# A two-layer memory-attention and gMLP kernel: where a piece of filler stands beside the output projection, and which engine runs Newton's steps of a LayerNorm

## The chip, the cores and the metric

The kernel runs on one core of a Trainium2 chip. The metric is device time in microseconds (us): the median of three runs before the change is 1888.75 us (1885.54 to 1890.63). A core has a matrix engine (PE), a vector engine (DVE), an activation engine (ACT), GpSimd (POOL) and a queue engine for transfers (SP). Each takes its instructions in the order of its own list and waits for the others by semaphores.

## The reference

The input x has 2048 rows of 512 bf16 numbers. Two layers follow each other, and each layer is an attention block (A) and a gated MLP (B), both with a residual:

```
for s in range(64):                       # A: 64 segments of 32 rows, one after another
    h = concat([mem, x_ln[32*s : 32*s+32]])            # 8 memory rows + 32 tokens
    q, k, v = h @ Wq, h @ Wk, h @ Wv                   # 32 heads of 128
    p = softmax(where(mask, q @ k.T * scale, -1e9))    # 40 x 40 per head
    o = (p @ v) @ Wo
    mem, out[s] = o[:8], o[8:]            # memory rows feed the next segment
x = x + out

z  = gelu(LN(x) @ w_in)                   # B: 2048 x 1376
z1, z2 = z[:, :688], LN(z[:, 688:])       # LN over the 688 columns
x  = x + (z1 * (w_sp @ z2 + b_sp)) @ w_out    # w_sp is 2048 x 2048
```

The memory rows make the segments of A a chain: segment s+1 can't start its projections before the first 8 rows of segment s have been through Wo. The LayerNorm of the second half of z needs, for each row, a mean, a variance and 1/sqrt(variance + eps).

## The kernel before

Each layer calls `a_block` (line 476) and then `b_block` (line 224).

**Order.** PE, DVE and ACT run in the order of the program text: `ORDERED` (line 28) is handed to `manual_schedule` (lines 425, 508, 238). In `b_block` SP is in that set too (line 238). POOL is not in it, so there a scheduler places POOL's instructions among each other.

**Attention segments.** `segment` (line 650) does one segment: projections of q and k by `mm_chunk` (line 527, matmuls on line 531), scores (line 688), the value projection `v_mm`, the products with the values (line 711), the sums of the softmax in `psD` (line 763), and then the product of the memory rows with Wo, `wo_pass` (line 582), whose 128 small matmuls all have line 586. Before Wo, DVE must have scaled the memory rows into `uT` (line 773). After Wo, DVE puts the memory rows into the next segment's input (`build_hA`, line 638: a predicated copy on line 641 and a transpose on line 642), behind `tok_out(0)` (line 721) in its order; ACT copies Wo's result `pw` out for storage (line 647). The result `pw` and the sums `psM` share one bank of the accumulation memory (`accB`), and the filler uses the other (`accA`).

**Filler.** At five places of a segment `fill()` takes one piece of independent work for PE: after `v_mm(0)` (line 740), after `v_mm(1)` (747), after `psD` (765), in the middle of Wo (778) and after `build_hA` (791). There are two kinds of pieces:

- `b_units` (line 557), in three of every four segments (`j4` = 1, 2, 3) while a next block of four segments exists: six chunks of 16 matmuls project the token rows of the next block. Every second chunk is cut in four pieces of 4 matmuls, the others come whole, so that the 15 pieces fill the five places of three segments. With whole chunks at the last place and quarters at the first four, each segment does two chunks.
- `y_part` (line 602), in the segment with `j4` = 0 from the fifth block on: 8 matmuls of 128x128x512 (line 598, `wo_last`) that put older token rows through Wo. The first four places get one matmul each, the last gets four.

So 45 segments of a layer carry `b_units`, 12 carry `y_part`, and 7 carry nothing.

**The gMLP's projection phase.** `b_block` begins with 16 calls of `project` (line 258), one for each tile of 128 rows. A projection is 12 matmuls (line 263) into one of two `pz` buffers of the accumulation memory, two gelus on ACT (lines 265, 266) that free this buffer, and three statistics instructions on DVE (lines 270 to 272). After every second tile `norms` (line 274) computes 1/sqrt(var + eps) for the pair with `_rstd_dve` (line 116): a starting value by integer arithmetic on the bits and three Newton steps, 12 small DVE instructions on 128x2 or 128x4 numbers, and one more for `nb` = -mean/std (line 282). `normalise` (line 286, on ACT) scales the tile by these; it is called for the pair of tiles before the present one, right after `norms`. So ACT's order reads: gelus of tiles 4 and 5 stand behind the normalise of tiles 0 and 1, and so on by pairs.

**The late rows.** The last four tiles of 128 rows (12 to 15) have not got their residual when A ends. POOL issues transfers for them at the start of `b_block`: `late_load` (line 250) loads the old x and A's output (`y_load`, line 199) and calls `y_add` (line 208), which adds the two on POOL (line 210) and stores the sum (line 211). Ahead of them stand POOL's two transfers of `w_out` (lines 290, 291), which is first used in `finish` (line 354), after the projection phase. In `norms` of pairs 2 and 3 (`tt` = 5 and 7) DVE also takes statistics of two late rows each; these share the Newton steps (n = 4), and `y_norm` (line 216) normalises them on DVE and stores them to `xb_d` through POOL's queue (line 221). SP then reads them back transposed for the last four projections (`load_rows`, line 156).

Of the kernel before, what the change touches and what calls it, by code (L numbers as in the profile page):

```python
# [10 lines left out]
ALU = mybir.AluOpType  # L11
# [104 lines left out]
def _rstd_dve(nc, pool, out, var, n):  # L116

    t = pool.tile([P, n], F32, name=f"nt{n}")
    nc.vector.tensor_scalar(out=t[:], in0=var, scalar1=LN_EPS, scalar2=None, op0=ALU.add)
    b = pool.tile([P, n], mybir.dt.int32, name=f"nb{n}")  # L120
    nc.vector.tensor_scalar(out=b[:], in0=t[:].bitcast(mybir.dt.int32), scalar1=-0.5, scalar2=float(0x5f3759df), op0=ALU.mult, op1=ALU.add)
    nc.vector.tensor_scalar(out=t[:], in0=t[:], scalar1=-0.5, scalar2=None, op0=ALU.mult)
    y = b[:].bitcast(F32)
    for k in range(3):
        q = pool.tile([P, n], F32, name=f"nq{n}")
        nc.vector.tensor_tensor(out=q[:], in0=y, in1=y, op=ALU.mult)
        nc.vector.tensor_tensor(out=q[:], in0=q[:], in1=t[:], op=ALU.mult)
        o = out if k == 2 else pool.tile([P, n], F32, name=f"ny{n}", bufs=2)[:]
        nc.vector.scalar_tensor_tensor(out=o, in0=q[:], scalar=1.5, in1=y, op0=ALU.add, op1=ALU.mult)
        y = o  # L130
# [93 lines left out]
def b_block(tc, c, rows, front, xd, MV_out, RS_out, w_sp, w_out, S, first, out_final=None):  # L224
# [4 lines left out]
    with ExitStack() as ctx:  # L229
# [8 lines left out]
        ctx.enter_context(tc.manual_schedule(engines=ORDERED | {mybir.EngineType.SP}))  # L238
# [11 lines left out]
        def late_load(tb, x=None, o=None):  # L250
            rows.y_load(tb, first, nc.gpsimd, x=x, o=o)
            rows.y_add(tb, first, nc.gpsimd, nc.gpsimd)
# [21 lines left out]
        def norms(q, late):  # L274

            n = 4 if late else 2
            for k, tb in enumerate(late):
                rows.y_stats(tb, mv[q][:, 2 + k, :])
            rs[q] = zp.tile([P, 4], F32, name="rs")
            nb[q] = zp.tile([P, 2], F32, name="nb")  # L280
            _rstd_dve(nc, zp, rs[q][:, 0:n], mv[q][:, 0:n, 1], n)
            nc.vector.scalar_tensor_tensor(out=nb[q][:], in0=mv[q][:, 0:2, 0], scalar=-1.0, in1=rs[q][:, 0:2], op0=ALU.mult, op1=ALU.mult)
            for k, tb in enumerate(late):
                rows.y_norm(tb, mv[q][:, 2 + k, 0:1], rs[q][:, 2 + k:3 + k], nc.gpsimd)
# [5 lines left out]
        nc.gpsimd.dma_start(w_out_sb[:, 0:5, :], w_out[0:640, :].rearrange("(fc p) d -> p fc d", p=P))  # L290
        nc.gpsimd.dma_start(w_out_sb[0:48, 5, :], w_out[640:688, :])
# [4 lines left out]
        late_load(NT - 1, wl[:, 0, :], wl[:, 1, :])  # L296
        for tt in range(NT):
            project(tt)
            if tt in (7, 9, 11):
                load_wsp((tt - 7) // 2)  # L300
            if tt == 14:
                load_x(0)
            if tt % 2 == 1:
                if tt // 2 + 3 < NT // 2:
                    front.load_rows(tt // 2 + 3)
                norms(tt // 2, {5: (NT - 4, NT - 3), 7: (NT - 2, NT - 1)}.get(tt, ()))
                if tt > 1:
                    normalise(tt - 3)
                    normalise(tt - 2)
# [166 lines left out]
def a_block(tc, c, rows, front, MV_in, RS_in, MV_out, RS_out, wqkv, Wo, S, first):  # L476
# [6 lines left out]
    with ExitStack() as ctx:  # L483
# [73 lines left out]
        def b_units(tb, early=False):  # L557
            bs = blk_state[tb]

            for k, j in enumerate((0, 2, 1, 3, 4, 5)):  # L560
                ps = (accA if k % 2 == 0 or not early else accB).tile([P, 512], F32, name="psb")
                for kts in (((0,), (1,), (2,), (3,)), ((0, 1, 2, 3),))[k % 2]:
# [39 lines left out]
        def y_part(G, q):  # L602

            pwB = accA.tile([P, DM], F32, name="pwB")
            for k, _ in enumerate(wo_last(G, range(8 * q, 8 * q + 8), pwB)):
                if k < 4:
                    yield
# [42 lines left out]
        def segment(s, fill, spare1, spare2, tail):  # L650
# [125 lines left out]
            wo_pass(pw, uT_cur, range(0, H // 2))  # L776

            fill()
            wo_pass(pw, uT_cur, range(H // 2, H))
# [116 lines left out]
```

The softmax here doesn't subtract the row's maximum and nothing guards it: scores larger than these inputs give would overflow.

## Time and profile before

The page and the trace below are of one profiled execution. It took 1885.15 us by the same clock as the runs, 3.6 us under their median; the span from its first to its last instruction is 1883.4 us.

| | us | share of the span |
|---|---|---|
| median of 3 runs | 1888.75 | |
| profiled execution | 1885.15 | |
| its span | 1883.4 | 100% |
| PE busy | 1761.1 | 94% |
| DVE busy | 1162.7 | 62% |
| ACT busy | 1120.7 | 60% |
| POOL busy | 136.6 | 7% |
| matmuls of Wo (line 586), busy | 286.1 | 15% |
| matmuls of the gMLP's projections (line 263), busy | 79.4 | 4% |
| transfers | 125.8 MB, 67 GB/s on average | |

The granted TensorE clock is 0.994 of full speed over the span, so no time differs by clock.

How to read the lines in the next part: a timeline line gives the start and the length of a group of like instructions in microseconds, the engine, the line of the kernel, the operation with what it writes and reads, its tile and how many there were. A square bracket at its end is the idle time of the engine just before, with the engine and the line of what ended it. PE's matmuls are pipelined, so the lengths of groups overlap slightly; differences of starts are safer than lengths. "issue" as a cause means that the engine waited for nothing that the profile shows. Line 531 is in `mm_chunk` and so stands for several callers: the tile tells them apart (`psb` is the filler `b_units`, `psm` a segment's own projection of q and k).

### The profile page before, as it was taken

To read this page: it belongs to the slowest core of one execution; us is meant where nothing else is said; L and a number is where in the kernel's file an instruction comes from. 1 tells how busy PE (TensorE), PEld (TensorE's weight loads), DVE (VectorE), ACT (ScalarE), POOL (GpSimd) and SP (SyncE) were. 2 spreads that over 40 slices of the span, in tenths; PEclk is the share of its full clock that TensorE was granted. 3 is DMA by queue.
4 is the path that set the end of the run, shared out by engine and by line. 5 is a ranking of instruction groups with operands and counts; after the bars stand their busy time and mean duration, and the time that the engine had idled before them with its cause. 6 is when DMAs were issued, how large, how long until landed. Compare 5 with 4: busy or idle time off the path is not lost.

```text
span 1883.4 us, 94288 instructions
## 1 busy us (share of the span) xinstructions
PE 1761.1 (94%) x43572; PEld 1015.0 (54%) x43596; DVE 1162.7 (62%) x2700; ACT 1120.7 (60%) x2074; POOL 136.6 (7%) x289
## 2 busy tenths in 40 slices
PE   3999999999999999889989999999999999998898
PEld 1555555555555555545545555555555555555455
DVE  1666666676667666674346666666766676665822
ACT  1666676666667666652036666666666666665600
POOL 5000000000000000032010000000000000001200
PEclk9999999999999999999999999999999999999999
DMA  9100000021002111267940000001210121114696
GB/s 348 46 19 19 20 18 18 21 68 38 17 17 72 42 25 39 78 154 162 207 139 21 21 21 21 21 21 32 80 35 21 32 83 39 29 43 124 141 186 130
DMA packets 189267, 125.80 MB, mean 67 GB/s; under 512 B 135896, under 2 KB 164328, under 8 KB 188872
## 3 DMA queue, kind: packets, MB, share of 16 engines
q1 hardware_dynamic: 167016, 71.01, 16.3%
q0 software_dynamic: 10560, 34.07, 5.5%
q10 hardware_dynamic: 11296, 14.70, 2.6%
q8 instruction: 340, 5.57, 1.2%
q14 instruction: 55, 0.45, 0.1%
HBM read 59.29 MB, written 33.56 MB: 49 GB/s over the span
## 4 chain that ended last, share of the span: by engine, by line
PE 84%; DVE 5%; DMA 4%; issue 3%; ACT 2%; POOL 0%; SPq 0%; ACTq 0%; DVEq 0%; POOLq 0%
PE psm L531 24%; PE pw L586 13%; PE psV L531 12%; PE psb L531 8%; PE pg L329 7%; PE psS L688 5%; PE psO L711 4%; PE pwB L598 3%; PE py L357 2%; PE psD L763 2%; PE pz L263 1%; PE psM L753 1%; DMA Wk_sb<-in_A_Wk_dram 1%; DVE uT L773 1%; DMA uT<-u 1%
## 5 line engine op out<-in xcount | busy, mean ns | idle before, releaser
L531 PEld LDWEIGHTS <-hA 128*32 128x32 bf16 x12288 | 306.4, 96 | 311.9 <-DVE hA L642 50.5
L667 ACT CAST rows<-psm 128x512 bf16<-128x512 f32 x512 | 299.8, 586 | 194.4 <-PE psm L531 194.4
L586 PE MATMUL pw<-Wo_sb,uT 128*32 128x128 bf16 x16640 | 286.1, 219 | 38.2 <-issue 25.9
L586 PEld LDWEIGHTS <-uT 128*32 128x32 bf16 x16640 | 245.2, 97 | 96.3 <-DVE uT L773 46.4
L531 PE MATMUL psm<-Wq_sb,hA 128*32 128x512 bf16 x4096 | 274.3, 382 | 11.7 <-DVE hA L642 9.1
L531 PE MATMUL psm<-Wk_sb,hA 128*32 128x512 bf16 x4096 | 269.9, 380 | 0.5 <-ACT rowsB L573 0.5
L531 PE MATMUL psV<-Wv_sb,hA 128*32 128x512 bf16 x4096 | 268.0, 382 | 0.0
L671 DVE STREAM_TRANSPOSE QQ<-rows 128x512 bf16<-128x512 bf16 x256 | 182.1, 711 | 80.6 <-ACT rows L667 79.0
L723 DVE TENSOR_TENSOR uT<-psO,Rt 128x384 bf16<-128x384 f32 x256 | 138.5, 541 | 119.7 <-ACT Rt L782 119.3
L692 ACT ACTIVATE E<-psS 128x448 bf16<-128x448 f32 x256 | 139.9, 547 | 117.8 <-PE psS L688 117.8
L671 DVE STREAM_TRANSPOSE KA<-rows 128x512 bf16<-128x512 bf16 x256 | 181.9, 710 | 38.3 <-ACT rows L667 35.6
L773 DVE TENSOR_TENSOR uT<-psO,Rm 128x128 bf16<-128x128 f32 x256 | 62.5, 286 | 164.3 <-PE psD L763 164.3
L782 ACT ACTIVATE Rt<-Rt 128x512 f32<-128x512 f32 x256 | 157.5, 629 | 4.1
L329 PE MATMUL pg<-z2n,wspT 128*128 128x344 bf16 x1024 | 154.8, 309 | 1.0 <-DVE u L337 1.0
L688 PEld LDWEIGHTS <-KA 128*64 128x64 bf16 x2048 | 79.7, 113 | 106.0 <-DVE KA L671 106.0
L531 PEld LDWEIGHTS <-hB 128*32 128x32 bf16 x3072 | 82.5, 98 | 97.5 <-issue 29.6
L771 ACT ACTIVATE Rt<-psD 128x1024 f32<-128x1024 f32 x128 | 131.1, 1024 | 6.0
L329 PEld LDWEIGHTS <-wspT 128*128 128x128 bf16 x1024 | 97.9, 98 | 54.2 <-issue 7.8
L531 PE MATMUL psb<-Wq_sb,hB 128*32 128x512 bf16 x1024 | 101.3, 396 | 26.9 <-DVE hB L546 26.9
L695 DVE TENSOR_TENSOR E<-E,maskN 128x448 bf16<-128x448 bf16 x256 | 95.3, 372 | 41.6 <-ACT E L692 41.6
L688 PE MATMUL psS<-QQ,KA 128*64 128x80 bf16 x2048 | 109.9, 208 | 1.1
L748 ACT CAST VA<-psV 128x512 bf16<-128x512 f32 x128 | 74.9, 585 | 56.7 <-PE psV L531 56.7
(147 smaller groups left out, 2229.4 us busy)
## 6 DMA issues: line engine op xcount, KB each, us to landing
Wo_sb<-in_A_Wo_dram POOLq DMA_DIRECT2D x8, 1024.0 KB, 13.1
xs<-xd ACTq DMA_DIRECT2D x32, 256.0 KB
o_d<-o_sb SPq DMA_DIRECT2D x126, 64.0 KB
y_o<-o_d SPq DMA_DIRECT2D x24, 256.0 KB
xd<-y_o SPq DMA_DIRECT2D x22, 256.0 KB
Wq_sb<-in_A_Wq_dram POOLq DMA_DIRECT2D x8, 512.0 KB, 8.0
Wk_sb<-in_A_Wk_dram POOLq DMA_DIRECT2D x8, 512.0 KB, 11.3
Wv_sb<-in_A_Wv_dram POOLq DMA_DIRECT2D x8, 512.0 KB, 10.7
```

The source lines that it names most:

```text
L329: nc.tensor.matmul(pg[t][:, k, 0:344], lhsT=wsp[t][:, st, :], rhs=z2n[:, st, 344 * k:344 * k + 344], start=(st == 0), stop=(st == NT - 1))
L531: nc.tensor.matmul(ps[32 * cg:32 * cg + 32, :], lhsT=lhs(kt, cg), rhs=rhs(kt, cg), start=(kt == 0), stop=(kt == KT - 1), tile_position=(0, ...
L586: nc.tensor.matmul(po[32 * cg:32 * cg + 32, 0:128], lhsT=lhs[:, n, :], rhs=wo_rhs(h, cg), start=(h == 0), stop=(h == H - 1), tile_position ...
L667: nc.scalar.copy(r[:], ps[:])
L671: nc.vector.transpose(out=QQ[:, j % 2, :, 0:32] if j < 2 else KA[:, j % 2], in_=r[:])
L688: nc.tensor.matmul(pS[64 * g:64 * g + 64, i, c0:80 if K is KA else 112], lhsT=K[:, r, n:n + 2, :].rearrange("p h k -> p (h k)"), rhs=q if ...
L692: nc.scalar.activation(out=E[:, r], in_=pS, func=ACT.Exp, scale=scale)
L695: nc.vector.tensor_tensor(out=E[:, r], in0=E[:, r], in1=maskN[:, j4, :].unsqueeze(1).to_broadcast([P, 4, 112]), op=ALU.mult)
L723: nc.vector.tensor_tensor(out=hview(uT_nxt[:], r, 8, 32), in0=oview(r, 8, 32), in1=Rr[:, :, :, 0:24], op=ALU.mult)
L771: nc.scalar.activation(out=Rt[:], in_=psD[:], func=ACT.Ln)
L773: nc.vector.tensor_tensor(out=hview(uT_cur[:], r, 0, 8), in0=oview(r, 0, 8), in1=Rm[:, :, r].rearrange("p g (n q) -> p g n q", q=8), op=AL ...
L782: nc.scalar.activation(out=rt, in_=rt, func=ACT.Exp, scale=-1.0)
```

## The change

Three edits.

1. The filler. `b_units` cuts its chunk in three pieces (4, 4 and 8 matmuls) in place of four, and `y_part` its eight matmuls in 1, 1, 2 and 4. The call of `fill()` in the middle of Wo is gone, and Wo runs in one piece. The piece after `psD`, ahead of Wo, is the one that is doubled.
2. Newton's steps. `_rstd_dve` becomes `_rstd_newton` with the engine as an argument, and `norms` calls it with POOL. The form that adds 1.5 and multiplies in one instruction is written as two, and `nb` as two, so that a pair's 13 DVE instructions become 17 on POOL. POOL is put into `manual_schedule` in `b_block` and runs in program order there. The adds of the late rows leave `late_load`: tiles 12 and 13 are added at `tt` = 1 just ahead of the first `norms`, tiles 14 and 15 at `tt` = 3 ahead of the second.
3. The two transfers of `w_out` are issued behind the loads of the late rows.

```diff
-def _rstd_dve(nc, pool, out, var, n):
+def _rstd_newton(eng, pool, out, var, n):
 
     t = pool.tile([P, n], F32, name=f"nt{n}")
-    nc.vector.tensor_scalar(out=t[:], in0=var, scalar1=LN_EPS, scalar2=None, op0=ALU.add)
+    eng.tensor_scalar(out=t[:], in0=var, scalar1=LN_EPS, scalar2=None, op0=ALU.add)
     b = pool.tile([P, n], mybir.dt.int32, name=f"nb{n}")
-    nc.vector.tensor_scalar(out=b[:], in0=t[:].bitcast(mybir.dt.int32), scalar1=-0.5, scalar2=float(0x5f3759df), op0=ALU.mult, op1=ALU.add)
-    nc.vector.tensor_scalar(out=t[:], in0=t[:], scalar1=-0.5, scalar2=None, op0=ALU.mult)
+    eng.tensor_scalar(out=b[:], in0=t[:].bitcast(mybir.dt.int32), scalar1=-0.5, scalar2=float(0x5f3759df), op0=ALU.mult, op1=ALU.add)
+    eng.tensor_scalar(out=t[:], in0=t[:], scalar1=-0.5, scalar2=None, op0=ALU.mult)
     y = b[:].bitcast(F32)
     for k in range(3):
         q = pool.tile([P, n], F32, name=f"nq{n}")
-        nc.vector.tensor_tensor(out=q[:], in0=y, in1=y, op=ALU.mult)
-        nc.vector.tensor_tensor(out=q[:], in0=q[:], in1=t[:], op=ALU.mult)
+        eng.tensor_tensor(out=q[:], in0=y, in1=y, op=ALU.mult)
+        eng.tensor_tensor(out=q[:], in0=q[:], in1=t[:], op=ALU.mult)
+        eng.tensor_scalar(out=q[:], in0=q[:], scalar1=1.5, scalar2=None, op0=ALU.add)
         o = out if k == 2 else pool.tile([P, n], F32, name=f"ny{n}", bufs=2)[:]
-        nc.vector.scalar_tensor_tensor(out=o, in0=q[:], scalar=1.5, in1=y, op0=ALU.add, op1=ALU.mult)
+        eng.tensor_tensor(out=o, in0=q[:], in1=y, op=ALU.mult)
         y = o
...
-        ctx.enter_context(tc.manual_schedule(engines=ORDERED | {mybir.EngineType.SP}))
+        ctx.enter_context(tc.manual_schedule(engines=ORDERED | {mybir.EngineType.SP, mybir.EngineType.Pool}))
...
         def late_load(tb, x=None, o=None):
             rows.y_load(tb, first, nc.gpsimd, x=x, o=o)
-            rows.y_add(tb, first, nc.gpsimd, nc.gpsimd)
...
-            _rstd_dve(nc, zp, rs[q][:, 0:n], mv[q][:, 0:n, 1], n)
-            nc.vector.scalar_tensor_tensor(out=nb[q][:], in0=mv[q][:, 0:2, 0], scalar=-1.0, in1=rs[q][:, 0:2], op0=ALU.mult, op1=ALU.mult)
+            _rstd_newton(nc.gpsimd, zp, rs[q][:, 0:n], mv[q][:, 0:n, 1], n)
+            nc.gpsimd.tensor_tensor(out=nb[q][:], in0=mv[q][:, 0:2, 0], in1=rs[q][:, 0:2], op=ALU.mult)
+            nc.gpsimd.tensor_scalar(out=nb[q][:], in0=nb[q][:], scalar1=-1.0, scalar2=None, op0=ALU.mult)
...
-        nc.gpsimd.dma_start(w_out_sb[:, 0:5, :], w_out[0:640, :].rearrange("(fc p) d -> p fc d", p=P))
-        nc.gpsimd.dma_start(w_out_sb[0:48, 5, :], w_out[640:688, :])
         late_load(NT - 4)
...
         late_load(NT - 1, wl[:, 0, :], wl[:, 1, :])
+        nc.gpsimd.dma_start(w_out_sb[:, 0:5, :], w_out[0:640, :].rearrange("(fc p) d -> p fc d", p=P))
+        nc.gpsimd.dma_start(w_out_sb[0:48, 5, :], w_out[640:688, :])
...
                 if tt // 2 + 3 < NT // 2:
                     front.load_rows(tt // 2 + 3)
+                if tt < 4:
+                    for k in range(2):
+                        rows.y_add(NT - 5 + tt + k, first, nc.gpsimd, nc.gpsimd)
                 norms(tt // 2, {5: (NT - 4, NT - 3), 7: (NT - 2, NT - 1)}.get(tt, ()))
...
-                for kts in (((0,), (1,), (2,), (3,)), ((0, 1, 2, 3),))[k % 2]:
+                for kts in (((0,), (1,), (2, 3)), ((0, 1, 2, 3),))[k % 2]:
...
             for k, _ in enumerate(wo_last(G, range(8 * q, 8 * q + 8), pwB)):
-                if k < 4:
+                if k in (0, 1, 3):
                     yield
...
             pw = accB.tile([P, 512], F32, name="pw")
-            wo_pass(pw, uT_cur, range(0, H // 2))
-
-            fill()
-            wo_pass(pw, uT_cur, range(H // 2, H))
+            wo_pass(pw, uT_cur)
```

Lines of the kernel after are shifted by what stands above them: line 531 becomes 535, 586 becomes 590, 598 becomes 602, 641 and 642 become 645 and 646.

## The prediction

> **What bounds the kernel now.** I read the page first (span, chain), then the waits, then the timeline of three kinds of attention segment, then the timeline of the two projection phases. The chain that ended last is mostly TensorE (PE):
>
> ```profile
> span 1883.4 us, 94288 instructions
> ...
> PE 84%; DVE 5%; DMA 4%; issue 3%; ACT 2%; POOL 0%; SPq 0%; ACTq 0%; DVEq 0%; POOLq 0%
> ```
>
> PE is the bound, but not at its peak: what can be won is the time in which PE stands between its own pieces of work. The change touches two such places.
>
> *Place 1: Wo in the attention segments.* One segment with filler from the next block's projection, from the timeline (PE, then DVE; columns: start, length in us, engine, line, work):
>
> ```profile
> 75.65 0.40 PE L531 MATMUL psb<-Wq_sb,hB 128*32 128x512 bf16 x4
> 76.09 1.08 PE L586 MATMUL pw<-Wo_sb,uT 128*32 128x128 bf16 x64
> 77.00 0.39 PE L531 MATMUL psb<-Wq_sb,hB 128*32 128x512 bf16 x4
> 77.21 1.07 PE L586 MATMUL pw<-Wo_sb,uT 128*32 128x128 bf16 x64
> ...
> 79.02 0.83 PE L531 MATMUL psm<-Wq_sb,hA 128*32 128x512 bf16 x12
> ...
> 75.75 0.49 DVE L773 TENSOR_TENSOR uT<-psO,Rm 128x128 bf16<-128x128 f32 x2 [1.41 <-PE psD L763]
> ...
> 78.33 0.29 DVE L641 CAST_PREDICATED pre<-maskM,pw 128x128 bf16<-128x128 uint16 x1
> ```
>
> A quarter chunk (4 matmuls) takes 0.21 us (77.00 to 77.21). The first one starts at 75.65, so PE is idle from about 75.87 until DVE has made uT and Wo starts at 76.09: a hole of 0.22 us. The second quarter stands in the middle of Wo. The next segment's first matmul comes 2.93 us after Wo's start (79.02). A segment without filler, same views:
>
> ```profile
> 99.24 1.97 PE L586 MATMUL pw<-Wo_sb,uT 128*32 128x128 bf16 x128 [0.36 <-DVE uT L773]
> 101.99 0.83 PE L531 MATMUL psm<-Wq_sb,hA 128*32 128x512 bf16 x12 [0.78 <-DVE hA L642]
> ...
> 101.31 0.28 DVE L641 CAST_PREDICATED pre<-maskM,pw 128x128 bf16<-128x128 uint16 x1
> ```
>
> Here Wo runs in one piece, and the next segment follows after 2.75 us, held by DVE (tok_out before build_hA), no longer by Wo. So 2.75 is the floor for 2.93. The segments whose filler is the old rows' Wo (y_part) pay more for the piece in the middle:
>
> ```profile
> 237.94 1.08 PE L586 MATMUL pw<-Wo_sb,uT 128*32 128x128 bf16 x64
> 238.96 0.39 PE L598 MATMUL pwB<-Wo_sb,front 128*128 128x512 bf16 x1
> 239.28 1.08 PE L586 MATMUL pw<-Wo_sb,uT 128*32 128x128 bf16 x64
> ```
>
> From the last small matmul to L598 0.15 us, from L598 to Wo again 0.32; the next segment starts at 241.25, 3.31 after Wo.
>
> *Place 2: the gMLP's projection.* 16 projections of 2.405 us (24 matmuls of two of them take 4.81) need 38.5 us of PE. They take 46.3 in layer 1 (807.60 to 853.92, the first gate matmul) and 43.4 in layer 2 (1733.48 to 1776.91): 7.8 and 4.9 us are lost. Why, in layer 1:
>
> ```profile
> 819.01 1.15 POOL L210 TENSOR_TENSOR y_o<-y_o,y_x 128x512 f32<-128x512 f32 x1 [3.52 <-DMA y_o<-o_d]
> 819.08 1.11 DVE L119 TENSOR_SCALAR nt<-mv 128x2 f32<-128x2 f32 x1
> 822.06 2.94 DVE L126 TENSOR_TENSOR nq<-ny 128x2 f32<-128x2 f32 x1
> 826.21 1.81 ACT L287 ACTIVATE z2n<-z,nb,rs 128x688 bf16<-128x688 f32 x2 [3.04 <-DVE nb L282]
> 829.33 6.49 PE L263 MATMUL pz<-front 128*128 128x512 bf16 x23 [2.98 <-ACT z L266]
> ```
>
> While GpSimd adds the late rows, three of DVE's Newton steps, 0.16 us elsewhere, last 1.11, 1.13 and 2.94. ACT waits for nb, PE for ACT. Later DVE (4.57 us per pair of tiles: 2.25 of statistics, 2.32 of Newton) stays just behind; in layer 2 the stretched step is one of 2.03 us.
>
> **The change, part by part.**
>
> *1. Filler ahead of Wo.* Nothing is added; 4 small matmuls (or one L598) go from the middle of Wo to the hole before it. In a projection segment the hole of 0.22 takes the 0.21, Wo ends 0.22 earlier, and the next start falls from 2.93 to the floor of 2.75, or 2.78 if ACT's copy of pw ends last (it follows one psum copy of 0.48 more than in the segment without filler). I take 0.165. The filler after Wo needs its bank, which ACT frees 1.93 after Wo's start (77.44+0.58 less 76.09); so it starts where it starts now, and ends in time. In a y_part segment the pause of 0.32 from L598 to Wo now comes before Wo (start 0.1 later), and 0.44 in the middle goes: 0.34.
>
> How many segments gain? Per layer 45 have projection filler and 12 y_part: 90 and 24. Going through the timeline, 47 and 18 run as shown; in the other 49 PE stands still in Wo or just after, which the waits call "issue" (39.8 us ahead of L586's weight loads). The instruction queue explains it: 340 packets of 16 KB, one per 256 PE instructions, and in the stalled segments PE resumes 1.2 to 1.6 us after the packet's end. There the time saved before the packet only lengthens the wait: 0. Full gain of the undisturbed: 47 x 0.165 + 18 x 0.34 = 13.9. By the same measure the next packet comes with less to spare than is saved in a good part of them, which takes some 2.5 off: **-11**. Ends: -8 (each hole 0.05 less useful) and -16.
>
> The Trainium skill ("Runtime: NRT & Kernel Launch", Instruction fetch mechanics) calls the cost of crossing a 16 KiB block "mostly hidden". By that rule all 114 segments would gain, 90 x 0.165 + 24 x 0.34 = 23 us; the "issue" rows speak against it, and I go by the rows.
>
> *2. Newton on GpSimd.* DVE loses 16 x 13 small instructions, 2.32 us per pair, and with them the stretched steps. GpSimd gets 16 x 17 (scalar_tensor_tensor becomes two), all but one dependent on the one before. No such instruction is in this trace. The nearest are the mask builds at the start, each waiting for the one before:
>
> ```profile
> 8.07 0.14 POOL L71 MEMSET maskf<- 32x64 f32 x1
> 8.28 0.27 POOL L74 TENSOR_SCALAR_AFFINE_SELECT maskf<-maskf 32x96 f32<-32x96 f32 x1
> 8.61 0.40 POOL L81 TENSOR_SCALAR_AFFINE_SELECT maskf<-maskf 32x32 f32<-32x32 f32 x2
> 9.08 0.40 POOL L79 TENSOR_SCALAR_AFFINE_SELECT maskf<-maskf 32x32 f32<-32x32 f32 x2
> ```
>
> Start to start 0.21 after a memset of 64 (0.16 without its elements), 0.33 after a select of 96 and 0.47 for a pair of 32 (about 0.25 for a lone one without elements). A tensor step reads two operands, a memset none: I take 0.22 per step, ends 0.12 (a memset of one element lasts 0.10) and 0.30. The chain is 16 x 0.22 + 0.25 = **3.8 us**, against 2.3 on DVE.
>
> Its place in the queue matters as much. GpSimd now runs in program order. In layer 1: the store of yB can go at 807.6 (ACT's copy ends at 807.54); the first o_d load waits for its landing, 3.5 us as now (808.45 to 811.95): 811.1. Seven loads of 0.54, w_out's 0.87 and 0.54: 816.3, by which time the first rows are there. Two adds of 1.16 with stores of 0.57: 819.8. Only then Newton(0), until 823.6; ACT wants it at 818.35 (the normalise after tile 3). What is queued behind ACT's wait is the gelus of tiles 4 and 5, and PE behind these: 823.65 + 1.81 of normalise + 0.64 + 0.73 of gelu puts projection 6 at 826.9, where unhindered it is at 807.6 + 3 x 4.81 = 822.0. Lost: 4.8. Then two more adds with stores (3.4), Newton(1) until 830.8, Newton(2) until 834.5. DVE's y_norm (tiles 12, 13) waits for that some 3.7 us, and behind it stand the statistics of tile 6 on, the two late-row statistics (1.86) and GpSimd's own stores of xb_d (2 x 0.55), which now precede Newton(3) in the same queue. Following the four engines forward so, projection 8 loses 2.4, 12 loses 2.8, 14 loses 1.9: 11.9 in place of 7.8, **+4.1**. Layer 2, the same walk with adds of 1.26 and the landing of the last rows some 17 us into the phase: 5.0 + 2.6 + 2.8 + 1.9 = 12.3 in place of 4.9, **+7.4**. Together +11.5. With 0.12 per step the walk gives -1, with 0.15 +2.5, with 0.18 +6, with 0.25 +16, with 0.30 +24.
>
> After the last projection the gate has 56 matmuls of 0.148 (8.3 us) before it needs tiles 14 and 15; Newton(7) and two normalises end 7.7 after the projections: covered, with 0.5 to spare at 0.22, and late by up to 0.8 per layer at 0.30 (not in the sums above).
>
> The Trainium skill ("GPSIMD Engine Reference", Engine selection) wants elementwise work on VectorE, GpSimd being about twice as slow with two inputs. The 128x512 add is the only pair in the trace: 1.15 to 1.28 us on POOL, 0.69 on DVE. By the rule, with twice DVE's step of 0.195, the walk would give +37 in place of +11.5.
>
> *3. w_out behind the late rows.* Same two issues (1.41 us), counted in the queue above. w_out lands at 818.0 now, some 4 later then; its first use is at 868 (py). Cost 0, covered by the gate's 14 us and the rest of the projections. The rows land earlier, which is worth nothing while GpSimd itself gets to them at 816.3.
>
> **Sum** against the profiled execution (1885.15 us, span 1883.4): -11 + 11.5 = +0.5. That execution lies 3.6 (0.2%) under the median of the runs, 1888.75; on that footing the forecast is 1889.2.
>
> **Rivals.** A measurement of this kernel tells about 0.3% (5.7 us) from no change.
>
> *The chain is short (faster).* DVE's own dependent steps come every 0.195; memset's 0.16 speaks for it, the selects against. From under 0.175 per step on, part 2 costs under 5.3 and the whole is faster; at 0.15: -11 + 2.5, 1880.
>
> *GpSimd becomes the bound of the projection (slower).* Place: Newton(0) to (3), where ACT, DVE's y_norm and the xb_d stores all wait for one queue. From 0.255 per step on part 2 costs over 16.7; at 0.28 some +20.5: 1898. For it: the selects' 0.25.
>
> *Wo's gain is eaten (slower).* If the instruction packets or ACT set the next segment everywhere, part 1 is worth 0: 1900. Against it: 47 segments at 2.93 exactly, those without filler at 2.75.
>
> *All filler segments gain (faster).* If the packets come earlier along with PE, -23: 1877. Against: resumption hangs on the packet, not on PE.
>
> **How the numbers follow.** Forecast (parts cancel within 5.7) 0.36; short chain 0.22; all segments gain 0.07; GpSimd bound 0.27; gain eaten 0.08. Faster 0.29, same 0.36, slower 0.35. The range runs from part 1 near its far end with a short chain (1888.75 - 14 + 2.5 = 1877) to part 1 as taken with a step of 0.30 (1888.75 - 11 + 24 = 1902), leaving about 0.2 outside; the likeliest case alone spans 1883 to 1894.5.
>
> **What would show it.** Right: L590 in one run of 128 with filler, next start 2.75 to 2.78 after Wo in undisturbed segments; y_part about 2.97; "issue" waits unchanged or a little longer; DVE free of stretched steps; ACT's z2n waiting about 5 us for POOL nb in each layer, projection 6 late; DVE's ln_xn waiting for POOL. Wrong: a step of Newton on POOL under 0.18 or over 0.25 us start to start; Newton(0) starting well before 12 us into the phase; Wo starting later because of the longer filler.

## The result and the profile after

The changed kernel takes 1890.86 us (median of 4 runs, 1887.11 to 1894.25), the kernel before 1888.17 (4 runs): a ratio of 1.0014, 95% interval 0.9990 to 1.0038. This can't be told from no change. On another chip, with 12 runs against 29, it was 1.0027 (1.0014 to 1.0040): some 5 us slower, just clear of no change.

The profiled execution took 1890.08 us. Its page, span and chain that ended last (compare PE's 84% and POOL's 0% before):

```profile
span 1888.4 us, 94381 instructions
...
PE 82%; DMA 5%; issue 4%; POOL 4%; DVE 3%; ACT 2%; ACTq 0%; SPq 0%; POOLq 0%; DVEq 0%
```

GpSimd is on the chain now. The 5 us of difference between the two spans are the rest of two large movements: in these two executions the projection phases of the two layers are 22.0 us longer, what lies ahead of and between them is 18.0 shorter, and what follows the second is 0.9 longer. *Place 1* is faster. The timeline of a segment with projection filler (start, length, engine, line, work):

```profile
76.52 0.61 PE L535 MATMUL psb<-Wq_sb,hB 128*32 128x512 bf16 x8
76.62 0.49 DVE L777 TENSOR_TENSOR uT<-psO,Rm 128x128 bf16<-128x128 f32 x2 [1.41 <-PE psD L767]
76.96 1.97 PE L590 MATMUL pw<-Wo_sb,uT 128*32 128x128 bf16 x128
...
79.02 0.28 DVE L645 CAST_PREDICATED pre<-maskM,pw 128x128 bf16<-128x128 uint16 x1
79.70 1.05 PE L535 MATMUL psm<-Wq_sb,hA 128*32 128x512 bf16 x16
```

The half chunk (76.52, eight matmuls) fills the hole, Wo follows in one run of 128, and the next segment starts 2.74 us after Wo (76.96 to 79.70), where it was 2.93. With y_part:

```profile
236.35 0.61 PE L602 MATMUL pwB<-Wo_sb,front 128*128 128x512 bf16 x2
236.89 1.97 PE L590 MATMUL pw<-Wo_sb,uT 128*32 128x128 bf16 x128
...
239.76 1.41 PE L535 MATMUL psm<-Wq_sb,hA 128*32 128x512 bf16 x16
```

2.87 after Wo in place of 3.31, and Wo itself starts 0.09 later.

*Place 2* is slower. The projections of layer 1, from the timeline of PE:

```profile
800.68 9.45 PE L263 MATMUL pz<-front 128*128 128x512 bf16 x47 [0.67 <-ACT yB L855]
809.97 4.81 PE L263 MATMUL pz<-front,ln_x 128*128 128x512 bf16 x23
821.42 6.41 PE L263 MATMUL pz<-front 128*128 128x512 bf16 x24 [6.64 <-ACT z L266]
830.29 6.49 PE L263 MATMUL pz<-front 128*128 128x512 bf16 x23 [2.47 <-ACT z L266]
836.62 4.81 PE L263 MATMUL pz<-front,ln_x 128*128 128x512 bf16 x24
844.38 6.49 PE L263 MATMUL pz<-front 128*128 128x512 bf16 x23 [2.94 <-ACT z L266]
851.67 4.81 PE L263 MATMUL pz<-front 128*128 128x512 bf16 x24 [0.80 <-ACT z L266]
856.42 9.79 PE L333 MATMUL pg<-z2n,wspT 128*128 128x344 bf16 x64
```

In layer 2 the phase begins and ends with these lines of PE, and PE's two longest pauses lie in between:

```profile
1724.95 4.81 PE L263 MATMUL pz<-front 128*128 128x512 bf16 x23 [0.68 <-ACT yB L855]
...
1745.80 6.72 PE L263 MATMUL pz<-front 128*128 128x512 bf16 x24 [6.12 <-ACT z L266]
1754.87 4.81 PE L263 MATMUL pz<-front 128*128 128x512 bf16 x23 [2.35 <-ACT z L266]
...
1768.94 7.09 PE L263 MATMUL pz<-front 128*128 128x512 bf16 x23 [4.34 <-ACT z L266]
...
1780.99 9.78 PE L333 MATMUL pg<-z2n,wspT 128*128 128x344 bf16 x64
```

ACT in layer 1:

```profile
818.30 1.81 ACT L288 ACTIVATE z2n<-z,nb,rs 128x688 bf16<-128x688 f32 x2 [6.75 <-POOL nb L283]
827.17 1.81 ACT L288 ACTIVATE z2n<-z,nb,rs 128x688 bf16<-128x688 f32 x2 [4.54 <-POOL nb L283]
```

From 800.68 to the first gate matmul at 856.42 it is 55.7 us, 46.3 before; layer 2 takes 56.0 (1724.95 to 1780.99), 43.4 before. PE waits for ACT (L266), ACT for nb. GpSimd's timeline shows what nb costs (the second add, the steps of pair 0, and the add behind them):

```profile
811.45 1.17 POOL L211 TENSOR_TENSOR xo<-xo,xs 128x512 f32<-128x512 f32 x1
812.92 0.56 POOL L212 DMA_DIRECT2D xd<-xo  x1 [0.30 <-POOL xo L211]
813.56 0.23 POOL L119 TENSOR_SCALAR nt<-mv 128x2 f32<-128x2 f32 x1
813.88 0.19 POOL L121 TENSOR_SCALAR nb<-nt 128x2 int32<-128x2 int32 x1
814.16 0.24 POOL L122 TENSOR_SCALAR nt<-nt 128x2 f32<-128x2 f32 x1
814.35 0.21 POOL L126 TENSOR_TENSOR nq<-nb 128x2 f32<-128x2 f32 x1
814.63 0.20 POOL L127 TENSOR_TENSOR nq<-nq,nt 128x2 f32<-128x2 f32 x1
814.92 0.22 POOL L128 TENSOR_SCALAR nq<-nq 128x2 f32<-128x2 f32 x1
...
818.04 0.22 POOL L283 TENSOR_SCALAR nb<-nb 128x2 f32<-128x2 f32 x1
818.22 1.16 POOL L211 TENSOR_TENSOR xs<-xs 128x512 f32<-128x512 f32 x1
```

17 steps from 813.56 to 818.26: 16 intervals of 0.28 us and a last step of 0.22, 4.7 in all. The steps shown last 0.19 to 0.24 themselves.

To weigh the two places apart I use two measures from each kernel's profiled execution: the length of each projection phase, and the stretch from the Wo of a layer's fifth attention segment to the Wo of its 63rd, summed over both layers. Each ratio is taken against runs of the kernel before on the same chip.

| kernel | ratio to before, 95% | phase 1 | phase 2 | attention stretch |
|---|---|---|---|---|
| before | 1 | 46.3 | 43.4 | 1364.6 |
| changed | 1.0014 (0.9990 to 1.0038) | 55.7 | 56.0 | 1349.3 |
| changed, again | 1.0027 (1.0014 to 1.0040) | 55.8 | 56.1 | 1348.6 |
| filler alone | 0.9934 (0.9912 to 0.9956) | 45.7 | 43.6 | 1349.0 |
| Newton, adds, w_out alone | 1.0133 (1.0106 to 1.0161) | 55.8 | 56.1 | 1361.5 |
| Newton back on DVE | 0.9928 (0.9904 to 0.9953) | 46.6 | 46.8 | 1344.2 |
| two steps on GpSimd | 0.9972 (0.9954 to 0.9990) | 50.1 | 50.4 | 1344.3 |
| idle matmuls in the pauses | 1.0020 (1.0003 to 1.0037) | 57.3 | 56.1 | 1347.0 |
| half chunk elsewhere | 0.9976 (0.9965 to 0.9987) | 46.4 | 47.3 | 1355.9 |
| filler, two steps on DVE | 0.9885 (0.9866 to 0.9905) | 43.3 | 44.5 | 1350.2 |
| adds behind the steps | 1.0026 (1.0015 to 1.0037) | 57.2 | 56.0 | 1349.8 |
| adds on DVE | 0.9989 (0.9977 to 1.0000) | 52.0 | 52.4 | 1351.1 |
| late rows set aside | 0.9939 (0.9921 to 0.9957) | 45.8 | 48.1 | 1351.5 |

By the stretch the filler is worth about 14.5 us: 1363.0 on average for the two kernels with the old filler, 1348.5 for the ten with the new ("half chunk elsewhere" left out). Those ten run the same attention code and still spread from 1344.2 to 1351.5, and the other two differ by 3.1, so I take the 14.5 as good to some 4 us, an estimate from these spreads. The phases with three Newton steps and the adds on GpSimd ahead of them repeat far better, within 0.1 us over three kernels. The phases of the changed kernel cost 111.8, against 89.8 in the profile of before (+22.0); the gate's start-up adds 0.2 in layer 1 and 0.9 in layer 2 (0.6 and 0.15 in the second profile of the same kernel).

### The profile page after: what moved, and what is told of

The parts are those of the page before. It is cut to its first block, busy times and chain, and to the rows that moved or that the text cites. A ratio compares the mean times of both kernels' runs of the same rounds, so it can differ in the third digit from the quotient of the medians.

```text
span 1888.4 us, 94381 instructions
## 1 busy us (share of the span) xinstructions
PE 1748.6 (93%) x43572; PEld 1008.6 (53%) x43596; DVE 1120.5 (59%) x2492; ACT 1112.7 (59%) x2074; POOL 193.8 (10%) x561
## 4 chain that ended last, share of the span: by engine, by line
PE 82%; DMA 5%; issue 4%; POOL 4%; DVE 3%; ACT 2%; ACTq 0%; SPq 0%; POOLq 0%; DVEq 0%
PE psm L535 23%; PE pw L590 12%; PE psV L535 12%; PE psb L535 10%; PE pg L333 7%; PE psS L692 5%; PE psO L715 4%; PE pwB L602 3%; PE py L361 2%; PE psD L767 2%; PE psM L757 1%; PE pz L263 1%; DMA Wo_sb<-in_A_Wo_dram 1%; DMA o_d<-yB 1%; DMA y_o<-o_d 1%
## 5 line engine op out<-in xcount | busy, mean ns | idle before, releaser
L590 PE MATMUL pw<-Wo_sb,uT 128*32 128x128 bf16 x16640 | 266.7, 219 | 41.1 <-issue 31.1
L590 PEld LDWEIGHTS <-uT 128*32 128x32 bf16 x16640 | 236.2, 97 | 90.6 <-DVE uT L777 49.5
L535 PE MATMUL psb<-Wq_sb,hB 128*32 128x512 bf16 x1024 | 90.4, 393 | 27.0 <-DVE hB L550 27.0
## 6 DMA issues: line engine op xcount, KB each, us to landing
Wk_sb<-in_A_Wk_dram POOLq DMA_DIRECT2D x8, 512.0 KB, 12.2
Wv_sb<-in_A_Wv_dram POOLq DMA_DIRECT2D x8, 512.0 KB, 11.5
```

The lines of the kernel that those rows point to most:

```text
L535: nc.tensor.matmul(ps[32 * cg:32 * cg + 32, :], lhsT=lhs(kt, cg), rhs=rhs(kt, cg), start=(kt == 0), stop=(kt == KT - 1), tile_position=(0, ...
L590: nc.tensor.matmul(po[32 * cg:32 * cg + 32, 0:128], lhsT=lhs[:, n, :], rhs=wo_rhs(h, cg), start=(h == 0), stop=(h == H - 1), tile_position ...
```

## The experiments

Theory after the profile of the changed kernel: both effects are larger than forecast, and cancel.

**The filler alone.** The kernel before with the first edit only:

```diff
-                for kts in (((0,), (1,), (2,), (3,)), ((0, 1, 2, 3),))[k % 2]:
+                for kts in (((0,), (1,), (2, 3)), ((0, 1, 2, 3),))[k % 2]:
...
-                if k < 4:
+                if k in (0, 1, 3):
...
-            wo_pass(pw, uT_cur, range(0, H // 2))
-
-            fill()
-            wo_pass(pw, uT_cur, range(H // 2, H))
+            wo_pass(pw, uT_cur)
```

> The first edit alone. Theory after the profile of the changed kernel: two effects larger than forecast cancel, the filler being worth -16 (from the first segment's Wo to the last, 1.5 of late start taken off) and the projection phases +22. Then this run is 16 us faster than before: ratio 0.9915, about 1872, with projection phases of 46 and 43.5 as before. Rival 1, the forecast's own step: -11, 0.994, 1877. Rival 2, the earlier segments of that profile are an accident of one execution (instruction packets): under -5, 1884 or more.

Measured: 0.9934, 8 to 17 us faster; phases as before; the attention stretch 15.6 shorter. By the time, 12 us at the middle of its interval, the forecast's -11 and the -16 can't be told apart; the stretch speaks for the larger. The accident of one execution is out.

**Newton, the adds' places and w_out alone.** The changed kernel with that first edit undone (the same lines, the other way round).

> The second and third edits alone, filler as before. Theory: phases of 55.7 and 56.0 in place of 46.3 and 43.4, the time +22, ratio 1.0115, about 1910. Rival, the forecast's own step: +11.5, 1.006, 1900. If this and the filler alone do not add up to the changed kernel's +2.7, the two edits disturb each other.

Measured: 1.0133 (1.0106 to 1.0161), 20 to 30 us slower, phases 55.8 and 56.1. The forecast's +11.5 is out. The two ratios add to 1.0067 where the changed kernel had 1.0014; so it was run again.

**The changed kernel again.**

> The changed kernel again, unaltered, on the chip of this call. The two edits alone gave 0.9934 [0.9912, 0.9956] and 1.0133 [1.0106, 1.0161], which add to 1.0067 +- 0.0035; the changed kernel gave 1.0014 [0.999, 1.0038]. Theory (they add, and the intervals are only wide): 1.001 to 1.005 here. Rival (the filler is worth more when GpSimd has the steps, or the reverse): outside of that, with phases or attention blocks that differ by more than 3 us from those of the two alone.

Measured: 1.0027 (1.0014 to 1.0040), in the range of the theory, though this interval only just meets that of the sum (1.0032 to 1.0102). Phases agree with those of Newton alone to 0.1 us, the attention stretch with that of the filler alone to 0.4: nothing in the traces says that the two edits touch each other. What differs from execution to execution lies elsewhere: PE's waits for the transposed u between the two layers are 1.5 us in the first profile of the changed kernel, 7.2 in the second and 4.0 in that of before, by the waits of PE between the first py and the next block.

**Newton back on DVE.** All else as in the changed kernel.

```diff
-            _rstd_newton(nc.gpsimd, zp, rs[q][:, 0:n], mv[q][:, 0:n, 1], n)
-            nc.gpsimd.tensor_tensor(out=nb[q][:], in0=mv[q][:, 0:2, 0], in1=rs[q][:, 0:2], op=ALU.mult)
-            nc.gpsimd.tensor_scalar(out=nb[q][:], in0=nb[q][:], scalar1=-1.0, scalar2=None, op0=ALU.mult)
+            _rstd_dve(nc, zp, rs[q][:, 0:n], mv[q][:, 0:n, 1], n)
+            nc.vector.scalar_tensor_tensor(out=nb[q][:], in0=mv[q][:, 0:2, 0], scalar=-1.0, in1=rs[q][:, 0:2], op0=ALU.mult, op1=ALU.mult)
```

> The changed kernel with Newton's steps and nb back on DVE; GpSimd keeps its program order, the adds at tt 1 and 3, w_out behind the late rows, and the new filler. Theory: the engine of the steps is the whole loss: phases back to 45 +- 1.5, the time equal to that of the filler alone within 3 us (about 1872, ratio 0.9915). Rival: the place of the adds and of w_out in GpSimd's queue carries a good part of it: phases over 49, time over 1880.

Measured: 0.9928, 1870.78 us, beside 1871.69 for the filler alone: the engine of the steps is the loss. The phases, 46.6 and 46.8, are a little above the 45 +- 1.5 of the theory, but not clearly above those of the other kernels with three steps on DVE (45.7 to 46.4 in layer 1, 43.4 to 47.3 in layer 2). The adds still hold up steps of DVE, now those of the first pairs. The timeline of DVE and POOL in layer 2:

```profile
1721.89 1.28 POOL L210 TENSOR_TENSOR y_o<-y_o,y_x 128x512 f32<-128x512 f32 x1
1721.91 1.30 DVE L122 TENSOR_SCALAR nt<-nt 128x2 f32<-128x2 f32 x1
1723.12 0.15 DVE L126 TENSOR_TENSOR nq<-nb 128x2 f32<-128x2 f32 x1
```

A DVE step of 0.17 us becomes 1.30 beside an add of 1.28, and ends when the add ends.

**Two steps in place of three.** The changed kernel with a shorter chain on GpSimd:

```diff
-    for k in range(3):
+    for k in range(2):
...
-        o = out if k == 2 else pool.tile([P, n], F32, name=f"ny{n}", bufs=2)[:]
+        o = out if k == 1 else pool.tile([P, n], F32, name=f"ny{n}", bufs=2)[:]
```

> The changed kernel with two Newton steps in place of three, so 13 GpSimd instructions per pair in place of 17 (this leaves out a refinement of 1/sqrt, whose error is then some 5e-6). At 0.28 us a step the chain falls from 4.7 to 3.6. Theory (the serial chain on GpSimd sets the phase): five chains stand one behind the other on the path, up to projection 12, so each phase falls by 5 x 1.12 = 5.6, the time by 11 (8 to 16 if slow-clock stretches go too): 1880, ratio 0.9955. Rival (the adds ahead in the queue and the landing of late rows set it): 1.1 to 2 per phase, 1887.

Measured: phases 50.1 and 50.4, 5.7 and 5.6 shorter than 55.7 and 56.0; the expectation said 5.6. The time, 1878.10 us, is 0.9972 of before. The four steps less shorten a chain by 1.12, and in layer 1 projection 6 starts 1.16 earlier, 8 2.30, 12 4.59, and the gate 5.67: one, two, four and five chains. So five chains stand one behind the other on the path, and each step of GpSimd counts five times per layer. The rival (the adds ahead, the landing of rows) is out.

**Adds behind the steps.** If GpSimd's list is the path, its order inside the list can't matter much.

```diff
+                norms(tt // 2, {5: (NT - 4, NT - 3), 7: (NT - 2, NT - 1)}.get(tt, ()))
                 if tt < 4:
                     for k in range(2):
                         rows.y_add(NT - 5 + tt + k, first, nc.gpsimd, nc.gpsimd)
-                norms(tt // 2, {5: (NT - 4, NT - 3), 7: (NT - 2, NT - 1)}.get(tt, ()))
```

> The changed kernel with GpSimd's adds of the late rows behind Newton's steps of the same tt (12 and 13 behind the first chain, 14 and 15 behind the second), and not ahead of them. In the changed kernel GpSimd never waits from its first add to the end of the third chain. Theory (its serial list up to the third chain sets the phase, in whatever order): projection 6 starts 4.2 us earlier (16.6 after the phase's start in place of 20.8), projection 8 4.5 earlier (25.1), but the third chain ends only 0.8 earlier, so the phases lose no more than 1 us each: time 1 to 2 us under the changed kernel. Rival (the first chain's place in the queue sets it): 4 us per phase, 8 in all.

Measured: projection 6 starts 16.6 after the phase's start (expected 16.6), projection 8 at 25.4 (25.1), and the phases are 57.2 and 56.0, not shorter; 1.0026 of before. Projections 6 to 9 come 4.2 us earlier, and this is given back by projections 10 and 12, from PE's timeline:

```profile
818.76 6.49 PE L263 MATMUL pz<-front 128*128 128x512 bf16 x24 [2.50 <-ACT z L266]
827.60 4.81 PE L263 MATMUL pz<-front 128*128 128x512 bf16 x23 [2.35 <-ACT z L266]
836.59 6.49 PE L263 MATMUL pz<-front,ln_x 128*128 128x512 bf16 x24 [4.18 <-ACT z L266]
```

The pause of 6.64 before projection 6 is 2.50 here, but projection 10 (836.59), which did not wait in the changed kernel, waits 4.18 and starts 34.4 after the phase's start (35.9 there); projection 12 starts at 43.6 (43.7). The third chain ends 31.3 after the phase's start, 31.4 in the changed kernel: 0.1 earlier where 0.8 was expected.

**Adds on DVE.** The same list, shortened by the four adds:

```diff
-                        rows.y_add(NT - 5 + tt + k, first, nc.gpsimd, nc.gpsimd)
+                        rows.y_add(NT - 5 + tt + k, first, nc.vector, nc.gpsimd)
```

> The changed kernel with the four adds of the late rows on DVE (0.69 us each there), the stores still on GpSimd. Theory (the serial list of GpSimd): 1.2 to 1.3 us per add leave it, so the chains come earlier by 2.3 (first), 5.2 (second and third), less in layer 2 where DVE has to wait for the rows: phases of some 50.5 and 52, 9 us faster than the changed kernel, 0.998 of before. Rival (the chain's length alone counts, or DVE's wait for the rows takes its place): phases over 54.

Measured: phases 52.0 and 52.4 (expected 50.5 and 52), 0.9989 (0.9977 to 1.0000): both phases are 3.7 shorter than those of the changed kernel, 7.4 in all where 9 were expected. The direction and the reason hold; layer 1 was taken 1.5 too low.

**Idle matmuls in the pauses.** After some pauses PE's first matmuls take twice as long, and the 24 of two projections 6.41 (821.42 above) in place of 4.81. The windows of PE show the granted clock there (window, length, busy, clock, DMA share, GB/s):

```profile
815.00:818.00 3.00, 0.00 (x0) 0.98 1.12 233
818.00:821.00 3.00, 0.00 (x0) 0.50 1.21 234
821.00:823.00 2.00, 1.58 (x4) 0.50 1.25 338
823.00:825.00 2.00, 2.00 (x7) 0.57 0.38 146
825.00:828.00 3.00, 2.83 (x16) 1.00 0.02 5
```

The forecast had no term for this, and the five such stretches of both layers add up to 9.2 us of matmul time. So PE was kept busy in the pauses:

```diff
+        def warm(n):
+            junk = one.tile([P, DM], F32, name="junk")
+            for i in range(n):
+                nc.tensor.matmul(junk[:], lhsT=w_in_sb[:, 0, 0:P], rhs=w_in_sb[:, 0, 0:DM], start=True, stop=True)
+
         def project(tt):
...
+            if tt in (6, 8, 12):
+                warm({6: 24, 8: 8, 12: 10}[tt])
```

> The changed kernel with idle matmuls (24, 8 and 10 of 128x512 on the weights, into a bank that nobody reads) ahead of projections 6, 8 and 12, where PE waits 6.1 to 6.6, 2.4 and 2.9 to 4.3 us and afterwards runs at a granted clock of 0.50. They take 4.8, 1.6 and 2.0 us of these pauses. The five slow stretches together add 9.2 us of matmul time. Theory A (they are a term of the +22, but only where projections 6 and 7 hold up tile 7's statistics and with them the fourth chain on GpSimd): clock 1.0 after projection 6, 3 to 4 us faster than the changed kernel, phases 54. Theory B (all of it on the path): 9 us. Theory C (GpSimd hides it all): 0. If the clock stays at 0.50 behind the idle matmuls, the pause is not what sets it.

Measured: 1.0020 (1.0003 to 1.0037), not to be told from the changed kernel. Projections 6 and 7 run at full clock, from PE's timeline of layer 1:

```profile
815.68 5.34 PE L261 MATMUL junk<-front 128*128 128x512 bf16 x24
822.46 4.81 PE L270 MATMUL pz<-front 128*128 128x512 bf16 x24 [1.44 <-ACT z L273]
827.10 1.89 PE L261 MATMUL junk<-front 128*128 128x512 bf16 x8
831.33 6.49 PE L270 MATMUL pz<-front 128*128 128x512 bf16 x24 [2.34 <-ACT z L273]
...
852.71 6.49 PE L270 MATMUL pz<-front 128*128 128x512 bf16 x24 [2.49 <-ACT z L273]
859.04 3.23 PE L340 MATMUL pg<-z2n,wspT 128*128 128x344 bf16 x21
```

But projections 6, 8, 12 and 14 start 20.7, 29.6, 43.7 and 51.0 after the phase's start, as in the changed kernel (20.7, 29.6, 43.7, 51.0) to the tenth; layer 2 too keeps its starts, with projections 6 and 12 at full clock and 8 now slow. So theory C: GpSimd sets the starts, and the slow clock is spent in time that PE would wait anyway. Only the last projections are on PE's own path: here the pause before projection 14 grew from 0.80 to 2.49, these two ran slowly, and the phase ended 1.5 later, at 57.3. The same 6.49 stands before the end in the kernel with the adds behind the steps (57.2).

**The half chunk elsewhere.** What pays in the filler: the hole ahead of Wo, or Wo in one piece?

```diff
-                for kts in (((0,), (1,), (2, 3)), ((0, 1, 2, 3),))[k % 2]:
+                for kts in (((0,), (1, 2), (3,)), ((0, 1, 2, 3),))[k % 2]:
```

> The filler alone, but the doubled piece of the projection filler stands after the second value projection and one quarter ahead of Wo; Wo in one piece, y_part as in the change. Theory (what pays is the hole of 0.21 ahead of Wo): the hole stays open and the quarter delays the product with the values by 0.21, so the 90 projection segments gain nothing and the 24 of y_part some 5 in all: 0.997 of before, 8 to 11 us slower than the filler alone. Rival (Wo in one piece is what pays, wherever the quarter goes): equal to the filler alone, 0.993.

Measured: 0.9976 (0.9965 to 0.9987), expected 0.997; the attention stretch is 6.9 above that of the filler alone. The next segment still starts 2.74 after Wo, but Wo starts later by the quarter (0.22 in the median of the projection segments). So the hole pays. The 7 us that are left in the stretch (1355.9 against 1363.0) fit y_part's share, 24 x 0.35 = 8.4.

**Two steps on DVE.** The filler alone with the shorter chain (the two lines of "two steps" above, in `_rstd_dve`).

> The filler alone, with two Newton steps in place of three, on DVE (one refinement of 1/sqrt is left out, error some 5e-6). DVE's pair falls from 4.57 to 3.98 us, under PE's 4.81. Theory (DVE's chain, ACT behind it, sets the pauses of the phase before the change): phases of 43 and 41 in place of 45.8 and 43.6, 5 us faster than the filler alone, 0.991 of before. Rival (the late rows' statistics, 1.86 us, and the adds of GpSimd set them): 1 to 2 us per phase at most, not to be told from the filler alone.

Measured: 0.9885 (0.9866 to 0.9905), 1868.11 us, the fastest version here. Phase 1 falls from 45.7 to 43.3, as expected. Phase 2 has 44.5, where PE waits 4.38 us ahead of projection 6 for the transfer of its rows in this execution (front from xb_d), not for DVE. Phases of kernels with DVE's steps vary by some 4 us in layer 2 (43.4, 43.6, 47.3) from one execution to another, so the phases alone don't give the gain. The two ratios, 0.9934 and 0.9885, differ by 0.0049, which is 9 us where 5 were expected and where the phases together are only 1.6 shorter; this size rests on two intervals of 0.4% from two chips and is not settled. That the version is faster than the filler alone is the theory's direction.

**Late rows set aside.** A version of its own: own tiles' two steps on DVE ahead of the late rows' statistics, the late rows' steps on GpSimd, their normalisation a pair later. A part of the edit (the new helpers are left out here):

```diff
+                if tt in (7, 9):
+                    late_norm(NT + tt - 11)
                 if tt // 2 + 3 < NT // 2:
                     front.load_rows(tt // 2 + 3)
...
-                norms(tt // 2, {5: (NT - 4, NT - 3), 7: (NT - 2, NT - 1)}.get(tt, ()))
+                norms(tt // 2)
+                if tt in (5, 7):
+                    late_stats(NT + tt - 9)
```

> A version of its own: the new filler; the steps of a pair's own tiles on DVE, two in place of three (one refinement is left out), right behind its statistics; the late rows' statistics behind these, their two steps alone on GpSimd, where a chain of 13 x 0.28 = 3.6 us has two pairs' time, and their normalisation one pair later. GpSimd in program order, adds at tt 1 and 3. DVE then has 3.98 us per pair, and 1.5 more in the two late ones. Theory (with the late rows out of ACT's way no pause over 2 us is left but for the adds): phases of 41 +- 1, 3 us faster than two steps on DVE alone, 0.987 of before. Rival (the adds stretch DVE's steps anyway, or the late rows come too late for projections 12 to 14): phases of 44 or more, 0.989.

Measured: 0.9939, slower even than the rival's 0.989, with phases of 45.8 and 48.1. The late rows come too late. From the timeline of PE in layer 1:

```profile
827.68 4.81 PE L266 MATMUL pz<-front,ln_x 128*128 128x512 bf16 x24
836.52 6.33 PE L266 MATMUL pz<-front 128*128 128x512 bf16 x23 [4.03 <-DMA front<-xb_d]
```

Projection 12 waits 4.03 for its rows' transfer, and in layer 2 projections 8, 12 and 14 wait 1.96, 2.02 and 2.74 for theirs. What had been a wait for DVE became a wait for a landing.

## Why the prediction was right in its number, and where its steps failed

The forecast was 1889.2 and the measured time 1890.86, with "same" as the likeliest case. That the number came out right is in good part luck. Newton's term was +22 and not +11.5; the total stayed near zero because the filler's gain came out on the large side of its -11: -14.5 by the attention stretch, good to some 4, and -8 to -17 by the time of its own run, which does not rule out -11. The terms as measured add to 22.0 + 1.1 - 14.5 = +8.6, the totals were +2.7 and +5; the rest is within the spread of the stretch. By a sign of being wrong that the forecast itself had named, a Newton step of over 0.25 us from start to start, its price failed. Step by step:

- *The reading of the bound* held. PE's waits in the phases come from ACT, ACT's from nb; Wo's hole takes the quarter; the floor of 2.75 is reached (2.74).
- *Filler, per undisturbed segment*: 0.165 taken, 0.19 measured; y_part 0.34 taken, 0.44 - 0.09 = 0.35 measured.
- *Filler, how many segments gain*: this step is not borne out, and not settled either. It gave the 49 segments where PE stands still a gain of 0. Projection segments whose next start comes over 0.16 us late reach it 3.71 (before) and 3.63 us (Newton, adds, w_out alone) after Wo on average with the old filler, and 3.50 to 3.65 with the new: about 0.1 less, hardly more than kernels with the same filler differ by. All segments together shrank by 24.3 us from Wo to the next start, between the first profiles of the two kernels, and grew by 7.0 from there to the next Wo; the medians of that second part stay the same but for y_part's 0.09, so it is the stalls that grow there. (The two kernels with the old filler differ by 6.1 and 2.1 in these sums.) That "resumption hangs on the packet, not on PE" (a rival's "against") holds for the moment of resuming: 93% of PE's 42 longer "issue" waits (over 0.3 us) ahead of Wo in the trace of before end between 1.15 and 1.65 us after a packet's end. But the packets seem to follow PE: in that trace 74% of the 340 packets start within 1.3 us after one of PE's boundaries of 256 instructions, which lie 4.8 us apart in the median, where 32% would by chance. Where the count of 256 begins was chosen to fit best; the same place fits best in all 13 traces, with 74 to 84%. So a packet would mostly come earlier when PE does, which was not tried on the chip. "Mostly hidden" (the Trainium skill, "Runtime: NRT & Kernel Launch", Instruction fetch mechanics) would have given 23, the rows as I read them 11, the runs about 14.5.
- *Newton's price per step*: this is the term that was mis-sized, 0.22 taken and 0.28 measured. The bounds, 0.12 and 0.30, held; the choice between them did not. The lone selects (0.25) were the nearer row, since they read an operand, and the memset was not. The forecast's own list of prices had 16 us at 0.25 and 24 at 0.30; at 0.28 it gave 20.5, and the phases grew by 22.0. So the walk along the four engines was good, and the input was wrong. By the rule for two inputs (the Trainium skill, "GPSIMD Engine Reference", Engine selection) a step would have cost an estimated 0.39 and the change 37. Ten of the 17 steps have two inputs; at 128x2 elements GpSimd's step, of either kind, is 1.4 times DVE's 0.195, not twice.
- *The place in the queue*: Newton(0) was put at 12.2 us into the phase and started at 12.9. The difference is a term that was left out: between an add and its store GpSimd stands 0.30 us ("[0.30 <-POOL xo L211]" above), twice before Newton(0). The importance that the forecast gave to the place ("matters as much") is refuted: behind or ahead of the steps, the phases are the same.
- *The rival "GpSimd becomes the bound"* named this mechanism, its place and the point from which it decides, 0.255 a step. At 0.28 that point is passed, and the total stayed within 0.3% all the same. With the filler at 14.5 the point would have been 14.5 + 5.7 = 20.2, by the same list just under 0.28: the change lies at the edge.
- *DVE freed*: the stretched steps are gone from the changed kernel, and this is worth nothing there, since DVE waits for GpSimd (21.8 us in four waits for rs).
- *w_out* cost nothing: first py 14.6 us after the first gate matmul in layer 1, 14.4 before. It was not tried by itself, but the kernel with Newton's steps back on DVE has it, at the time of the filler alone.
- *The gate's cover*: "late by up to 0.8 per layer at 0.30": 0.2 and 0.9 measured, 0.6 and 0.15 in the second profile.

The waits of the two kernels say the same in one line each, first of before, then of after (engine, tile and line, releaser, us in total, times, longest):

```profile
ACT z2n L287 <- DVE nb L282: 19.4, 10, 3.0
PE pz L263 <- ACT z L266: 10.9, 6, 3.0
```

```profile
ACT z2n L288 <- POOL nb L283: 44.9, 16, 6.8
PE pz L263 <- ACT z L266: 26.3, 9, 6.6
```

## What to carry to other kernels

Price a chain of dependent small instructions by the nearest row that reads an operand, count every step as often as chains stand one behind the other on the path, and move such a chain to another engine only if the steps there are as short: here 0.085 us more per step and four steps more per pair cost some 18 of the 22 us (phases of 111.8, 93.4 with the steps back on DVE). When a list of one engine is never idle from its first to its last piece, reordering it can move waits about and gain nothing, as here; shorten it. And where a forecast is near zero as the difference of two terms, run each alone: a right total says nothing of either.

## What the runs showed that was not expected

- *The clock after a pause.* The granted clock falls to 0.50 for 3.41 us, or twice that, after some pauses: behind 2.47 us in the changed kernel's layer 1 the 24 matmuls take 6.49, behind 2.35 in its layer 2 they take 4.81. Over all 13 traces, none of 19 pauses of 1 to 2 us ahead of a projection is followed by it, 19 of 31 of 2.0 to 3.4 us are, and all 22 of 4 us and more. Within a trace these stretches start whole multiples of 3.41 us apart (in the clock records of the changed kernel at 817.87, 831.53 and 845.18, four times 3.41 each), so where a pause lies on this grid seems to decide. The Trainium skill ("TensorE: Matmul & The Clock Gate", What's actually happening) has the clock halved after an idle window of about 3.4 us that runs free of the kernel; the grid agrees with a free-running window, but that 2.3 us can be enough is less than a whole one. The mean clock of 0.994 that was given ahead hides two such stretches in layer 1 of the kernel before, one of them behind its pause of 2.98 (829.33, 6.49 long).
- *Adds that hold DVE up.* Steps on DVE of 0.16 us last as long as GpSimd's 128x512 add beside them (1.30 beside 1.28), while statistics of 128x344 beside such an add keep their 0.50 (811.38 in the changed kernel, beside the add at 811.45). The Trainium skill ("SBUF — State Buffer", Who interferes with whom) has the two engines share a pair of ports that one instruction holds as a whole, and exempts instructions with one input outside the fast modes; the statistics agree with it. The TENSOR_SCALAR step that was held up has one input, so it agrees only if it ran in a fast mode, which no run here shows.
